# Tokens put in order by the copy out of the attention's banks, and one store per output tile or quarter in place of two

## The chip, the cores and the metric

The kernel runs on one core of a Trainium2 chip. The metric is the device time of one execution in microseconds. Three runs of the kernel before gave 297.45 us as their median (295.93 to 299.62).

## The reference

A retention layer (attention with a decay in place of the softmax) feeds a feed-forward layer with a sine in it. Eight batches of eight heads, 576 tokens each, head width 64; the feed-forward layer has width 512 in and out and 2048 inside.

```
scores = (1/8) * q @ k.T                                  # per batch and head, 576 x 576
gamma[h] = 1 - 2 ** (-5 - h)
ret = scores * where(i >= j, gamma[h] ** (i - j), 0)
attn = ret @ v                                            # 576 x 64 per head
x = attn.transpose(0, 2, 1, 3).reshape(4608, 512)         # heads side by side, one row per token
h = x @ w_in                                              # 4608 x 2048
g = h + sin(alpha * h) ** 2 / (alpha + 1e-9)
out = g @ w_out                                           # 4608 x 512, float32
```

Inputs and output are float32; inside, the matmuls take 16-bit operands and add up in 32 bits.

## The kernel before, in words

The 576 tokens of a batch are two blocks (p = 0, 1) of 256 tokens and an end of 64. The ends of all eight batches are gathered to a ninth block of 512 tokens (class `Ends`), which the feed-forward layer takes as n = 8; n = 0 to 7 are the 512 tokens of batch n's two blocks.

**Token order.** A load of q, k or v of a block (line 158) puts two neighbouring tokens, r = 0 and 1, side by side on one partition, so that the DMA moves longer runs: partition 64 g + i holds the tokens 128 g + 2 i + r. The attention therefore works on tokens in the order (g, r, i): first a half's 64 even tokens, then its 64 odd ones. From batch 4 on (`HALVED`), k and v are loaded in another order (line 153), and half of the masked scores' columns for r = 1 are left out (`i0` = 32 in `scores` and `values`).

**Attention.** `scores` fills a PSUM tile, `masked` multiplies it with the mask into a 16-bit tile, `values` (matmul at line 427) multiplies with v, and `add_states` (line 449) adds what the earlier chunks of 128 tokens contribute through their running state. Both write the tile `o`: two banks (t = 0, 1) of 512 columns, each 2 x 2 x 128 for head pair x, half g and 128 tokens (r, i). They are matmuls of 64 x 64 that use a quarter of the array each. `keep` copies a block's two banks to `xT`, the feed-forward layer's 16-bit input, with ScalarE (line 120) or VectorE (line 122). Columns keep their order on the way.

**Feed-forward layer.** `project` (line 562) makes 16 chunks of 128 hidden features per block, `sine` and `square` (lines 570 and 579 on ScalarE, 581 on the others) and `product` (line 586, VectorE) make `gT`, and the second product follows. For n = 0 to 2 that is `gemm2` (line 605), one tile of 128 tokens by 512 columns at a time, copied out and stored by `finish`. For n = 3 to 8 it is seven products instead of eight in Strassen's manner (`part_product`, line 671; sums at lines 642 and 652), whose results are quarters of 256 tokens by 256 columns, added up on VectorE (line 718) and stored by `store`.

**Stores.** A tile of 128 output rows has the even tokens on its first 64 partitions and the odd ones on the others. So `finish` (line 598) and `store` (line 688) start two transfers each, one for r = 0 and one for r = 1, each to every second row of the output. For n = 8 the two halves belong to different batches (line 684).

**Order of the work.** It is written out by hand, instruction by instruction, for the first three blocks, and as lists of steps per unit for the others. All loads, all transposes by DMA (line 230) and nearly all stores are issued by SP, in program order. Eight completion semaphores are used in turn for these transfers, so that each one waits for the transfer eight places before it. The tile `osb`, from which the stores read, has four buffers.

Of the kernel before, what the change touches and what calls it, by code (L numbers as in the profile page):

```python
# [10 lines left out]
F32 = mybir.dt.float32  # L11
# [25 lines left out]
def kernel(  # L37
# [18 lines left out]
    nc = tc.nc  # L56

    B, H, S, D = q.shape
    DM, FF = moe_w_in.shape
    NT = out.shape[0]  # L60
    P = 128
# [23 lines left out]
    work = ctx.enter_context(tc.tile_pool(name="w", bufs=1))  # L85
# [29 lines left out]
    def halves(n):  # L115
        return slice(64 * n, 64 * n + 64)

    def copy(eng, d_, s_):
        if eng is nc.scalar:
            eng.copy(d_, s_)  # L120
        else:
            eng.tensor_copy(d_, s_)  # L122
# [136 lines left out]
    def change_rows(key):  # L259

        if key in open_turns:
            nc.tensor.drain()
            open_turns.clear()

    def order(later, earlier):
        tc.add_manual_dep(
            later.ins,
            earlier.ins.name,
            mybir.DependencyInfo(mybir.DependencyClass.Sync, mybir.DependencyReason.DATA),
            reason="rows of the two halves take turns at a bank",  # L270
        )

    def told(last, eng):

        mark = eng.nop()
        order(mark, last)
        return mark

    class Attention:
        def __init__(self, b):  # L280
            self.b = b
            self.halved = b >= HALVED
            self.both = {}
            self.o = {}
            self.ret = {}
            self.sc = {}
            self.kv = {}
            self.tiles = {}
            self.mark = {}
# [115 lines left out]
        def values(self, p, same, *tags, relay=None):  # L405

            if same:
                change_rows((self, p))
            else:
                if relay is None:  # L410
                    open_turns.append((self, p))
                if len(tags) == 2:
                    self.o[p] = [psum.tile([P, 512], F32, tag=tag, bufs=1, name="o") for tag in tags]
                else:
                    self.both[p] = psum.tile([P, 2, 512], F32, tag=tags[0], bufs=1, name="o")
                    self.o[p] = [self.both[p][:, t] for t in range(2)]
            o, v16 = self.o[p], half[self.b, "v", p]
            made = []
            for x in range(2):
                for r in range(2):  # L420
                    i0, n = (32, 64) if self.halved and r else (0, 128)
                    for e in range(2):
                        for g in range(2):
                            t = g if same else 1 - g
                            c = 256 * x + 128 * g
                            m = 256 * e + 128 * r
                            made.append(matmul(
                                o[t][halves(e), c : c + 128].rearrange("p (r i) -> p r i", r=2)[:, :, i0:64],
                                v16[halves(g), 4 * t + 2 * x + e, r, :],
                                self.ret[p, x][halves(g), t, m : m + n],  # L430
                                start=(not same and x == 0 and r == 0), stop=False, skip_group_check=True,
                            ))
            if not same and relay is not None:
                self.mark[p] = told(made[-1], relay)
            elif p in self.mark:
                order(made[0], self.mark[p])

        def add_states(self, p, gs=(0, 1)):
            o, qT = self.o[p], T[self.b, "q", p]
            for g in gs:  # L440
                if 2 * p + g == 0:
                    continue
                st = self.state_of(2 * p + g - 1)
                for x in range(2):
                    for e in range(2):
                        for t in range(2):
                            a = 2 * x + e
                            c = 256 * x + 128 * g
                            matmul(
                                o[t][halves(e), c : c + 128],  # L450
                                st[halves(t), a, :],
                                qT[halves(t), 2 * a : 2 * a + 2, halves(g)],
                                start=False, stop=True, skip_group_check=True,
                            )

        def keep(self, p, *engs):

            cols = slice(256 * p, 256 * p + 256)
            if len(engs) == 1:
                copy(  # L460
                    engs[0],
                    self.x[:, :, cols].rearrange("p (t x) n -> p t x n", t=2),
                    self.both[p].rearrange("p t (x n) -> p t x n", x=2),
                )
                return
            for t, eng in enumerate(engs):
                copy(eng, self.x[:, 2 * t : 2 * t + 2, cols], self.o[p][t].rearrange("p (x n) -> p x n", x=2))

    class Ends:

# [75 lines left out]
    ops = {}  # L546
# [38 lines left out]
        hps, ss_t = hps_of.pop((n, fc))  # L585
        nc.vector.scalar_tensor_tensor(gT[n][:, fc, :], ss_t, inva[:, fc : fc + 1], hps, MULT, ADD)  # L586

    def rows_of(n, c):
        if n == 8:
            return out.rearrange("(b s) d -> b s d", s=S)[2 * c : 2 * c + 2, 512:576, :]  # L590
        r0 = 576 * n + 128 * c
        return out[r0 : r0 + 128, :].rearrange("(i r) d -> r i d", r=2)

    def finish(n, c, eng=None, cols=slice(0, 512), issue=(nc.sync, nc.sync)):
        osb = work.tile([P, 512], F32, tag="osb", bufs=4, name="osb")
        copy(eng or nc.scalar, osb[:, cols], ops[n, c, cols.start][:, cols])
        for r in range(2):
            issue[r].dma_start(rows_of(n, c)[r, :, cols], osb[halves(r), cols])

    def gemm2(n, u, tag, cols=slice(0, 512)):  # L600
        c, part = divmod(u, 4)
# [74 lines left out]

    def store(n, t, e, osb, js=(0, 1), issue=(nc.sync, nc.sync)):
        cols = slice(256 * e, 256 * e + 256)
        for r in range(2):
            if n == 8:  # L680
                b0 = 4 * t + 2 * js[0]
                dst = out.rearrange("(b s) d -> b s d", s=S)[b0 : b0 + 2 * len(js), 512:576, cols]
                dst = dst.rearrange("(j r) s d -> r s j d", r=2)
                issue[r].dma_start(dst[r], osb[halves(r), js[0] : js[-1] + 1])
            else:
                r0 = 576 * n + 256 * t + 128 * js[0]
                dst = out[r0 : r0 + 128 * len(js), cols].rearrange("(j i r) d -> r i j d", r=2, i=64)
                issue[r].dma_start(dst[r], osb[halves(r), js[0] : js[-1] + 1])

    kept = {}  # L690

# [8 lines left out]
    def after_product(n, i, js=(0, 1), issue=(nc.sync, nc.sync), apart=False, more=False):  # L700
        acc = parts[n, i]
        if i == 1:
            nc.scalar.copy(kept_tile("low"), acc)
        elif i == 6:
            nc.vector.tensor_tensor(kept_tile("mid"), acc, kept["low"], ADD)
        elif i == 7:
            nc.vector.tensor_tensor(kept["low"], acc, kept["mid" if apart else "low"], ADD)
        else:
            t, e = {2: (0, 0), 3: (0, 1), 4: (1, 0), 5: (1, 1)}[i]
            cols = slice(256 * js[0], 256 * js[-1] + 256)  # L710
            if (n, i) not in kept:
                kept[n, i] = work.tile([P, 2, 256], F32, tag="osb", bufs=4, name="osb")
            osb = kept[n, i].rearrange("p j d -> p (j d)")
            source = kept["mid" if i == 3 else "low"]
            if i == 2 and not apart:
                nc.scalar.copy(osb[:, cols], acc[:, cols])
            else:
                nc.vector.tensor_tensor(osb[:, cols], acc[:, cols], source[:, cols], ADD)  # L718
            store(n, t, e, kept[n, i], js, issue)
            if more:  # L720
                nc.vector.tensor_tensor(kept["mid"], acc, kept["mid"], ADD)
# [60 lines left out]
    with tc.manual_schedule():  # L782
# [222 lines left out]
        load(4, "v", 0)  # L1005
        load(3, "q", 1)
        finish(0, 1)
        at[1].to_state(2, A_)
        finish(0, 3)
        at[1].values(1, True)  # L1010
        at[1].add_states(1)
# [393 lines left out]
        n = NBLK - 1  # L1405
# [50 lines left out]
```

## Time and profile before

| | |
|---|---|
| median of three runs | 297.45 us (295.93 to 299.62) |
| the profiled execution | 296.62 us |
| its span | 294.9 us |
| TensorE (PE), VectorE (DVE), ScalarE (ACT), GpSimd (POOL) busy | 283.0, 225.4, 204.1, 135.8 us |
| granted TensorE clock | 1.0 |
| written to and read from HBM | 9.44 MB, 36.75 MB |
| stores of 128 KB issued by SP | 67 |

PE stands for matmuls, PEld for weight loads beside them. L427 is line 427 of the kernel. SPq is SP's queue of transfers; the time of an issue there is that of the issuing instruction, not of the transfer. In a row of a group, the number behind "x" is the count, then come the busy time of all and the mean of one in ns, and behind the second bar the idle time ahead of them. In a row of waits "A <- B: 1.4, 1, 1.4" A waited for B, 1.4 us in total, once, at most 1.4 us.

### The profile page before, as it was taken

How to read it: one execution, taken by the hardware profiler on the slowest of the kernel's cores; microseconds unless marked ns; L12 is line 12 of the kernel's file. 1: busy time of each engine (PE TensorE's matmuls, PEld its weight loads, DVE VectorE, ACT ScalarE, POOL GpSimd, SP SyncE). 2: the span in 40 equal slices, each digit the busy share in tenths (PEclk: the TensorE clock that was granted, in tenths of full speed). 3: DMA queues.
4: the chain of work that ended last, by engine and by line, in shares of the span. 5: the costliest groups of instructions: out<-in, count | busy, mean ns of one | idle time of the engine just before them, and what ended most of it. 6: DMA issues, size and time to landing. Idle time of an engine off the chain costs nothing. (4 is left out here: it accounts for less than half of the span.)

```text
span 294.9 us, 8502 instructions
## 1 busy us (share of the span) xinstructions
PE 283.0 (96%) x3480; PEld 183.2 (62%) x3480; DVE 225.4 (76%) x336; ACT 204.1 (69%) x341; POOL 135.8 (46%) x151
## 2 busy tenths in 40 slices
PE   6789999999998999999999999999999999999994
PEld 4556545555544554455767766776667776777783
DVE  2586978788347979687987698769877987987884
ACT  2668935998594796787866986688668657765510
POOL 5684678655687684570298129802970000000000
PEclk9999999999999999999999999999999999999999
DMA  7999999998798778997987968798764103110313
GB/s 218 347 234 211 246 291 317 263 261 232 172 204 187 166 165 179 256 174 166 162 192 207 171 148 196 212 147 168 181 151 113 40 10 81 36 38 21 83 39 109
DMA packets 123431, 50.09 MB, mean 170 GB/s; under 512 B 80384, under 2 KB 121344, under 8 KB 123392
## 3 DMA queue, kind: packets, MB, share of 16 engines
q1 hardware_dynamic: 119440, 44.78, 65.5%
q0 software_dynamic: 2688, 4.19, 7.8%
q10 hardware_dynamic: 1264, 0.58, 0.7%
q8 instruction: 27, 0.44, 0.6%
q14 instruction: 12, 0.10, 0.1%
HBM read 36.75 MB, written 9.44 MB: 157 GB/s over the span
## 5 line engine op out<-in xcount | busy, mean ns | idle before, releaser
L586 DVE SCALAR_TENSOR_TENSOR gT<-ss,inva,hps 128x512 f16<-128x512 f16 x144 | 105.6, 744 | 31.5 <-ACT ss L579 27.9
L570 ACT ACTIVATE s<-hps,alpha_t 128x512 f16<-128x512 f32 x144 | 96.8, 680 | 47.1 <-PE hps L562 46.7
L562 PE MATMUL hps<-xT,w_in 128*128 128x512 f16 (+1 forms) x532 | 121.1, 372 | 0.8 <-DMA w_in<-in_moe_w_in_dram 0.8
L562 PEld LDWEIGHTS <-w_in 128*128 128x128 f16 x596 | 66.6, 114 | 50.2 <-DMA w_in<-in_moe_w_in_dram 1.1
L579 ACT ACTIVATE ss<-s 128x512 f16<-128x512 f16 x107 | 67.2, 630 | 2.8
L605 PE MATMUL ops<-w_out,gT 128*128 128x512 f16 x192 | 46.8, 380 | 0.0
L671 PEld LDWEIGHTS <-gT 128*128 128x128 f16 x384 | 37.5, 98 | 8.3
L207 POOL TENSOR_TENSOR k<-raw,cn 128x1024 f16<-128x1024 f32 (+1 forms) x17 | 29.5, 1738 | 9.1 <-DMA raw<-in_k_dram 9.0
L671 PEld LDWEIGHTS <-S 128*128 128x128 f16 x288 | 27.7, 98 | 5.3
L605 PEld LDWEIGHTS <-gT 128*128 128x128 f16 x192 | 17.9, 98 | 20.4
L359 POOL TENSOR_TENSOR s<-kvs,cn 128x256 f16<-128x256 f32 x17 | 10.4, 612 | 40.1 <-DVE S L652 36.6
L207 POOL TENSOR_TENSOR q<-raw,cn 128x1024 f16<-128x1024 f32 x13 | 24.6, 1900 | 7.1 <-DMA raw<-in_q_dram 4.7
L671 PE MATMUL hps<-T,gT 128*128 128x256 f16 x192 | 22.9, 273 | 0.0
L671 PE MATMUL hps<-w_out,gT 128*128 128x256 f16 x192 | 22.9, 273 | 0.0
L671 PE MATMUL hps<-w_out,S 128*128 128x256 f16 x192 | 22.8, 273 | 0.0
L397 DVE TENSOR_TENSOR ret<-sc,mask 128x1024 f16<-128x1024 f32 x16 | 19.1, 1218 | 2.3 <-PE sc L385 2.2
L367 POOL TENSOR_TENSOR kvs<-s,kvs 128x256 f32<-128x256 f32 x21 | 16.7, 797 | 3.6 <-DVE kvs L122 1.1
L718 DVE TENSOR_TENSOR osb<-hps,low 128x512 f32<-128x512 f32 x13 | 9.0, 691 | 9.6 <-PE hps L671 9.6
L581 DVE TENSOR_TENSOR ss<-s 128x512 f16<-128x512 f16 x29 | 13.4, 465 | 3.7 <-ACT s L570 3.7
L366 POOL TENSOR_TENSOR s<-kvs,cn 128x256 f32<-128x256 f32 x21 | 12.9, 612 | 6.8 <-ACT kvs L120 6.6
L652 DVE TENSOR_TENSOR S<-gT,S 128x1024 f16<-128x1024 f16 x24 | 15.5, 684 | 0.0
L397 DVE TENSOR_TENSOR ret<-sc,mask_halved 128x768 f16<-128x768 f32 x16 | 15.2, 950 | 0.0
(83 smaller groups left out, 269.5 us busy)
## 6 DMA issues: line engine op xcount, KB each, us to landing
out_dram<-osb SPq DMA_DIRECT2D x67, 128.0 KB, 2.5
raw<-in_q_dram SPq DMA_DIRECT2D x16, 512.0 KB, 5.1
raw<-in_k_dram SPq DMA_DIRECT2D x8, 512.0 KB, 6.1
raw<-in_v_dram SPq DMA_DIRECT2D x8, 512.0 KB, 6.0
raw<-in_v_dram SPq DMA_DIRECT2D x32, 128.0 KB, 3.3
raw<-in_k_dram SPq DMA_DIRECT2D x32, 128.0 KB, 3.1
w_in<-in_moe_w_in_dram POOLq DMA_DIRECT2D x4, 512.0 KB, 11.9
w_out<-in_moe_w_out_dram POOLq DMA_DIRECT2D x4, 512.0 KB, 13.2
```

The source lines that it names most:

```text
L207: eng.tensor_tensor(dst[:, a0:a1].rearrange("p a r t d -> p t (a r) d"), t_.rearrange("p (t a) x -> p t a x", t=2)[:, :, a0:a1].rearrange( ...
L366: nc.gpsimd.tensor_tensor(s32, self.kvs[:, c - 1], g1.unsqueeze(2).to_broadcast([P, 4, D]), MULT)
L367: nc.gpsimd.tensor_tensor(self.kvs[:, c], s32, self.kvs[:, c], ADD)
L397: nc.vector.tensor_tensor(ret.rearrange("p t (z x) -> p (t z) x", z=2)[:, :, 0:n], sc.rearrange("p t (z x) -> p (t z) x", z=2)[:, :, 0:n], ...
L562: matmul(hps_of[n, fc][0][:, cols], w_in16[fc // 4][:, a, fc % 4 :: 4], xs[n][:, a, cols], start=(a == 0 and part != 1), stop=(a == KT - 1 ...
L570: nc.scalar.activation(s_t, hps, mybir.ActivationFunctionType.Sin, bias=0.0, scale=alpha_t[:, fc : fc + 1],)
L579: nc.scalar.activation(ss_t, s_t, mybir.ActivationFunctionType.Square)
L581: eng.tensor_tensor(ss_t, s_t, s_t, MULT)
L586: nc.vector.scalar_tensor_tensor(gT[n][:, fc, :], ss_t, inva[:, fc : fc + 1], hps, MULT, ADD)
L605: matmul(ops[n, c, cols.start][:, cols], gT[n][:, fk, c * P : (c + 1) * P], w_out16[:, fk, cols], start=(fk == 0), stop=(fk == FC - 1), sk ...
L652: return eng.tensor_tensor(out_, x, y, op)
L671: matmul(acc[:, 256 * j : 256 * j + 256], lhs[:, x, 128 * j : 128 * j + 128], rhs[:, x], start=(tag is not None and j == js[0] and p == 0 ...
```

## The change

A new function `columns` gives the half g and head pair x of a bank a new place: the bank's 256 columns of a head pair are now ordered (r, g, i) instead of (g, r, i). `values` and `add_states` write their 128 columns through it, as two runs of 64 that lie 128 apart. `keep` reads runs of 128 columns (n = 64 g + i) and writes column n of r to place 2 n + r, so that `xT` holds the tokens in their own order. From there on a tile of 128 rows is 128 rows of the output one after the other, and `finish` and `store` start one transfer of 256 KB each. For n = 8 the two transfers stay.

```
+    def columns(bank_, x, g, e):
+        mine = bank_[halves(e), 256 * x : 256 * x + 256]
+        return mine.rearrange("p (r g i) -> p g r i", r=2, g=2)[:, g]
...
                             t = g if same else 1 - g
-                            c = 256 * x + 128 * g
                             m = 256 * e + 128 * r
                             made.append(matmul(
-                                o[t][halves(e), c : c + 128].rearrange("p (r i) -> p r i", r=2)[:, :, i0:64],
+                                columns(o[t], x, g, e)[:, :, i0:64],
...
                             a = 2 * x + e
-                            c = 256 * x + 128 * g
                             matmul(
-                                o[t][halves(e), c : c + 128],
+                                columns(o[t], x, g, e),
...
                 copy(
                     engs[0],
-                    self.x[:, :, cols].rearrange("p (t x) n -> p t x n", t=2),
-                    self.both[p].rearrange("p t (x n) -> p t x n", x=2),
+                    self.x[:, :, cols].rearrange("p k (n r) -> p k r n", r=2),
+                    self.both[p].rearrange("p t (x r n) -> p (t x) r n", x=2, r=2),
                 )
                 return
             for t, eng in enumerate(engs):
-                copy(eng, self.x[:, 2 * t : 2 * t + 2, cols], self.o[p][t].rearrange("p (x n) -> p x n", x=2))
+                copy(
+                    eng,
+                    self.x[:, 2 * t : 2 * t + 2, cols].rearrange("p x (n r) -> p x r n", r=2),
+                    self.o[p][t].rearrange("p (x r n) -> p x r n", x=2, r=2),
+                )
...
-    def finish(n, c, eng=None, cols=slice(0, 512), issue=(nc.sync, nc.sync)):
+    def finish(n, c, eng=None):
         osb = work.tile([P, 512], F32, tag="osb", bufs=4, name="osb")
-        copy(eng or nc.scalar, osb[:, cols], ops[n, c, cols.start][:, cols])
-        for r in range(2):
-            issue[r].dma_start(rows_of(n, c)[r, :, cols], osb[halves(r), cols])
+        copy(eng or nc.scalar, osb, ops[n, c, 0])
+        r0 = 576 * n + 128 * c
+        nc.sync.dma_start(out[r0 : r0 + 128, :], osb)
...
     def store(n, t, e, osb, js=(0, 1), issue=(nc.sync, nc.sync)):
         cols = slice(256 * e, 256 * e + 256)
-        for r in range(2):
-            if n == 8:
...
+        if n == 8:
...
+            for r in range(2):
                 issue[r].dma_start(dst[r], osb[halves(r), js[0] : js[-1] + 1])
-            else:
-                r0 = 576 * n + 256 * t + 128 * js[0]
-                dst = out[r0 : r0 + 128 * len(js), cols].rearrange("(j i r) d -> r i j d", r=2, i=64)
-                issue[r].dma_start(dst[r], osb[halves(r), js[0] : js[-1] + 1])
+        else:
+            r0 = 576 * n + 256 * t
+            nc.sync.dma_start(out[r0 : r0 + 256, cols].rearrange("(j p) d -> p j d", p=P), osb)
```

More of the change, by code (lines that the diff above doesn't have):

```diff
@@ L586, in product @@
         nc.vector.scalar_tensor_tensor(gT[n][:, fc, :], ss_t, inva[:, fc : fc + 1], hps, MULT, ADD)
-    def rows_of(n, c):
-        if n == 8:
-            return out.rearrange("(b s) d -> b s d", s=S)[2 * c : 2 * c + 2, 512:576, :]
+    def finish(n, c, eng=None):
+        osb = work.tile([P, 512], F32, tag="osb", bufs=4, name="osb")
+        copy(eng or nc.scalar, osb, ops[n, c, 0])
         r0 = 576 * n + 128 * c
-        return out[r0 : r0 + 128, :].rearrange("(i r) d -> r i d", r=2)
-    def finish(n, c, eng=None, cols=slice(0, 512), issue=(nc.sync, nc.sync)):
-        osb = work.tile([P, 512], F32, tag="osb", bufs=4, name="osb")
-        copy(eng or nc.scalar, osb[:, cols], ops[n, c, cols.start][:, cols])
-        for r in range(2):
-            issue[r].dma_start(rows_of(n, c)[r, :, cols], osb[halves(r), cols])
+        nc.sync.dma_start(out[r0 : r0 + 128, :], osb)
     def gemm2(n, u, tag, cols=slice(0, 512)):
@@ L678, in store @@
         cols = slice(256 * e, 256 * e + 256)
-        for r in range(2):
[L680 to L683, printed above, removed]
+        if n == 8:
+            b0 = 4 * t + 2 * js[0]
+            dst = out.rearrange("(b s) d -> b s d", s=S)[b0 : b0 + 2 * len(js), 512:576, cols]
+            dst = dst.rearrange("(j r) s d -> r s j d", r=2)
+            for r in range(2):
                 issue[r].dma_start(dst[r], osb[halves(r), js[0] : js[-1] + 1])
-            else:
-                r0 = 576 * n + 256 * t + 128 * js[0]
-                dst = out[r0 : r0 + 128 * len(js), cols].rearrange("(j i r) d -> r i j d", r=2, i=64)
-                issue[r].dma_start(dst[r], osb[halves(r), js[0] : js[-1] + 1])
+        else:
+            r0 = 576 * n + 256 * t
+            nc.sync.dma_start(out[r0 : r0 + 256, cols].rearrange("(j p) d -> p j d", p=P), osb)
     kept = {}
```

## The prediction

> **What bounds the kernel now.** I read the page's span and engine rows first, then the busy time of each engine by stage, then what TensorE waited for, then the timelines of SP, GpSimd and TensorE around the one wait that was found.
>
> ```profile
> span 294.9 us, 8502 instructions
> ...
> PE 283.0 (96%) x3480; PEld 183.2 (62%) x3480; DVE 225.4 (76%) x336; ACT 204.1 (69%) x341; POOL 135.8 (46%) x151
> ...
> 0.00:21.00 21.00, 15.28 (x300) 11.20 (x300) 12.52 (x24) 10.86 (x18) 14.89 (x24) 1.00 1.04 269
> 21.00:75.00 54.00, 53.44 (x733) 30.55 (x734) 42.70 (x63) 40.03 (x66) 33.74 (x35) 1.00 1.05 256
> 75.00:92.00 17.00, 15.62 (x102) 7.62 (x101) 7.54 (x12) 11.88 (x25) 13.07 (x12) 1.00 0.89 196
> 92.00:265.00 173.00, 172.77 (x2144) 113.44 (x2142) 141.51 (x206) 131.63 (x217) 74.06 (x83) 1.00 0.69 147
> 265.00:295.00 30.00, 25.90 (x206) 20.38 (x204) 21.14 (x34) 9.67 (x16) 0.00 (x0) 1.00 0.23 62
> ```
>
> A stage row gives its length, then busy time of PE, PEld, DVE, ACT and POOL, the granted clock (1.00 throughout) and the share of the DMA engines. PE's idle time is the length less the first busy number: 5.72 us in the start, 0.56 until 75 us, 1.38 between 75 and 92 us, 0.23 in the 173 us after that, 4.10 in the end. So TensorE sets the pace from 21 us on, and no edit of transfers or copies gains more than 0.56 + 1.38 + 0.23 = 2.17 us there. The start lies before the first store, and the stores of the last block (n == 8), which end the run, stay as they are: I leave both ends at nothing.
>
> What made PE wait between 21 and 290 us:
>
> ```profile
> PE sc L385 <- DMA qT<-q: 1.4, 1, 1.4
> PE hps L562 <- DMA w_in<-in_moe_w_in_dram: 0.8, 1, 0.8
> ```
>
> The second is a weight load ahead of all stores. The first is the wait of the stage 75 to 92 us. The three engines' timelines there (start, length, instructions):
>
> ```profile
> 68.36 4.25 SPq L598 DMA_DIRECT2D out_dram<-osb  x6
> ...
> 75.54 1.23 SPq L598 DMA_DIRECT2D out_dram<-osb  x2
> 76.87 2.99 SPq L153 DMA_DIRECT2D raw<-in_k_dram  x4
> 80.37 0.40 SPq L158 DMA_DIRECT2D raw<-in_q_dram  x1
> 80.88 2.76 SPq L230 DMA_TRANSPOSE kT<-k  x1
> ...
> 85.02 2.10 SPq L230 DMA_TRANSPOSE qT<-q  x1
> ...
> 76.18 1.06 ACT L120 CAST v<-raw 128x1024 f16<-128x1024 f32 x1
> ...
> 77.75 3.76 POOL L207 TENSOR_TENSOR q<-raw,cn 128x1024 f16<-128x1024 f32 x2
> ...
> 85.20 3.62 PE L605 MATMUL ops<-w_out,gT 128*128 128x512 f16 x16
> 90.19 0.64 PE L385 MATMUL sc<-qT,kT 64*64 64x128 f16 x32 [1.38 <-DMA qT<-q]
> ```
>
> SP issues one transfer behind the other here with hardly a gap. The scores of batch 3 need the transpose that SP issues at 85.02; TensorE is through with its other work at 88.8 us and starts at 90.19.
>
> **The stores.** Twelve tiles (n = 0 to 2, `finish`) and twenty quarters (n = 3 to 7, `store`) lose one of two transfers each: 32 issues on SP's queue. The order of all other instructions on the five engines stays.
>
> ```profile
> L688 SPq DMA_DIRECT2D out_dram<-osb x40: 595/610/1255, 152.2 to 278.3; - x40
> L598 SPq DMA_DIRECT2D out_dram<-osb x24: 517/592/1720, 68.4 to 146.0; - x24
> ...
> DMA to landing us min/median/max: 2.3/2.5/4.9
> ...
> L230 SPq DMA_TRANSPOSE qT<-q x12: 1242/1314/2476, 54.9 to 199.7; - x12
> ```
>
> 12 x 0.592 + 20 x 0.610 = 19.3 us of SP's issue time go, nearly all of it beside TensorE, so they are worth only what PE waited for SP. Of the eight stores ahead of the late transpose four go: three from the first row (3 x 4.25/6 = 2.1 us) and one from the third (0.6 us), together 2.7 us. May SP run that far ahead? The load at 80.37 waits for ScalarE's cast of v, over at 77.24, so it may start at 77.7. The transpose needs GpSimd's second cast of the row at 77.75, over at 81.5, so it may start at 82.3. Both conditions hold, so the transpose can land about 2.7 us earlier, at 87.5, ahead of the 88.8 at which TensorE comes for it. Gain: 1.38 us. The bounds are 0 (what shortens ahead of it is given back, since the issues at 80.88 and 85.02 took 2.76 and 2.10 us where the median transpose of q takes 1.31, so SP was perhaps held by the transfers in flight) and the whole 2.17 us of idle time. What is late next is the transpose of the other half of q of batch 3, which SP issues behind one more store pair; SP is further ahead there than TensorE would be, so I add nothing.
>
> A store of 256 KB instead of 128 KB is one issue with twice the rows. Its issue is bounded by 0.52 us (the shortest store) and by two of the old ones, 1.2 us; I take 0.6, because the issues with 64 and with 128 rows stand at 0.592 and 0.610. Its landing lies between the old store's 2.5 us and a 512 KB load's:
>
> ```profile
> raw<-in_k_dram SPq DMA_DIRECT2D x8, 512.0 KB, 6.1
> ```
>
> Who waits for a landing? The buffer `osb`, one of four, is rewritten a whole block later, and the program uses eight completion semaphores in turn, so each transfer waits for the one eight places before it. Eight issues with their gaps last 8 x 4.25/6 = 5.7 us, and loads of 6.1 us pass through the same ring now. I add nothing; if a store took as long as such a load, SP would stand for 6.1 - 5.7 = 0.4 us behind it, and TensorE not at all.
>
> **The copies.** `keep` now writes its 16-bit result with a step of two elements. The copies, and the nearest others (mean ns of one behind the bar):
>
> ```profile
> L120 ACT CAST xT<-o 128x1024 f16<-128x1024 f32 x10 | 10.1, 1018 | 0.0
> L120 ACT COPY kvs<-kv 128x512 f32<-128x512 f32 x9 | 5.2, 587 | 3.3 <-PE kv L321 2.7 <-PE o L427 0.6
> L120 ACT CAST xT<-o 128x512 f16<-128x512 f32 x5 | 2.8, 593 | 1.2 <-PE o L449 1.2
> L122 DVE CAST xT<-o 128x512 f16<-128x512 f32 x5 | 3.4, 686 | 0.1
> L122 DVE COPY osb<-ops 128x512 f32<-128x512 f32 x2 | 1.4, 686 | 2.3 <-PE ops L605 2.3
> L122 DVE CAST xT<-o 128x1024 f16<-128x1024 f32 x1 | 1.2, 1223 | 1.3 <-PE o L449 1.3
> ```
>
> No row has a step of two 2-byte elements. The nearest ones write 4-byte elements side by side, so 512 elements lie at the same pitch as they will now: 587 against 593 ns on ScalarE, 686 against 686 on VectorE. I take 0. The lower bound is 0 too, since nothing is taken off the copies; the upper one is a doubling, 10.1 + 2.8 + 3.4 + 1.2 = 17.5 us over two engines. On TensorE that would cost only where it comes at once for the copy:
>
> ```profile
> 19.40 1.27 DVE L122 CAST xT<-o 128x512 f16<-128x512 f32 x2
> 21.16 1.06 PE L562 MATMUL hps<-xT,w_in 128*128 128x256 f16 x8 [0.77 <-DMA w_in<-in_moe_w_in_dram]
> ...
> 48.90 1.00 ACT L120 CAST xT<-o 128x1024 f16<-128x1024 f32 x1
> 50.49 1.68 PE L562 MATMUL hps<-xT,w_in 128*128 128x512 f16 x7
> ```
>
> Batch 0: the pair would end about 22.1 instead of 20.67, 0.9 us after 21.16. Batch 1: 50.9 against 50.49, 0.4 us. Behind the later copies TensorE has other work first. Together 1.3 us.
>
> **The matmuls.** `values` and `add_states` now write two runs of 64 columns, 128 apart, instead of 128 in one run. No instruction is added. The rows:
>
> ```profile
> L427 PE MATMUL o<-ret,v 64*64 64x128 f16 x384 | 10.7, 221 | 0.5
> L449 PE MATMUL o<-qT,s 64*64 64x128 f16 x192 | 6.0, 218 | 0.1
> L427 PE MATMUL o<-ret,v 64*64 64x64 f16 x128 | 4.5, 190 | 0.0
> L385 PE MATMUL sc<-qT,kT 64*64 64x64 f16 x128 | 3.7, 189 | 0.0
> ...
> 100.13 1.38 PE L427 MATMUL o<-ret,v 64*64 64x128 f16 x64
> 101.34 0.51 PE L449 MATMUL o<-qT,s 64*64 64x128 f16 x24
> ```
>
> 384 + 192 = 576 matmuls change. The 128 of line 427 with 64 columns already write two runs, of 32 columns 64 apart (the half-masked batches, `i0` = 32), and take 190 ns; the same size of line 385, in one run, takes 189. So I take 0. The Trainium skill says otherwise: its page "PSUM — Partial Sum Buffer", section "Specifications (TRN2)", gives 8-byte cachelines there and has any non-contiguous pattern slow matmuls significantly. By that rule the attention's matmuls would stretch and the sum would be a loss instead of a gain; the rows of lines 427 and 385 speak against it at runs of 32.
>
> **Sum.** The profiled execution took 296.62 us, 1.72 us around its span. 296.62 - 1.38 + 0 + 0 = 295.2. It lies 0.83 us below the median of the runs shown, 297.45 (295.93 to 299.62); carried to a median that is 297.45 - 1.38 = 296.1, which I forecast.
>
> **Rivals.** A: nothing moves. SP gets ahead, but the transpose lands as late as before, because a transfer's landing is bound by the traffic (0.89 of the DMA engines in that stage), or TensorE waits as long at the next transpose. For it: SP's two long transposes. Against it: bytes and packets of the stores are unchanged, and they come earlier. 297.4 us.
>
> B, on the other side: the split output slows the 576 matmuls. 64 of them took 101.34 - 100.13 = 1.21 us, 19 ns each as four tiles of the array work together. If the second run costs as much again, 576 x 19 ns = 10.9 us on the bound engine: 297.4 + 10.9 = 308.3 (307 if the wait goes as well). It passes 2% (5.9 us) from 10 ns per matmul on. Against it stands the pair 190 and 189 ns.
>
> C: strided copies take up to double: +1.3 us, which eats the gain: 297.4 us. Against it: the equal rows at the same pitch.
>
> D: more is gained than TensorE's idle time between 21 and 265 us, over 2%. Nothing in the stage rows leaves room for it; below 291.5 us.
>
> **How the numbers follow.** Forecast (295 to 297) 0.57, A 0.26, C 0.06, B 0.08, D 0.03. All but B and D lie within 2%, about what a measurement of this kernel can tell from no change: same 0.89, slower 0.08, faster 0.03. The range goes from the lowest run shown less the largest gain, 295.93 - 2.17 = 293.8, to the highest run shown with no gain, 299.6; it holds A and C and leaves out B and D.
>
> **What would show it.** Stores: 12 at line 598 and 20 at the line of `store`, about 0.6 us each, 256 KB. The wait of `sc` for `qT` at 88 us gone or under 0.3 us, and 75 to 92 us with PE idle below 0.5 us. Copies to xT at 1.0 and 0.6 us on ScalarE, 0.69 on VectorE. Values and states at 215 to 225 ns, and 64 in a row in about 1.2 us. The prediction is wrong if PE's busy time grows (B), if the copies grow and `project` waits for them (C), or if a transfer waits where none did.

## The result, and the profile after

The changed kernel takes 296.39 us (median of 20 runs, 295.34 to 298.54), the kernel before took 298.55 us beside it (20 runs, 295.71 to 300.0). The ratio is 0.994, with a 95% interval of 0.9917 to 0.9963: a gain of 0.4 to 0.8%, within the 2% that count as no change. A second measurement of the same code gave 296.65 us (12 runs, 295.24 to 297.92) against 297.33, a ratio of 0.9975 (0.9951 to 1.0). The forecast was 296.1 us. The ratios here are worked out from fast runs alone (at most 1.5% above the fastest of the same kernel), so they need not be the quotient of the medians.

The profiled execution of the first measurement happened to be the slowest of its 20 runs, 298.54 us, so a profile of the second one (296.89 us, span 295.2) stands beside it below, as the second profile. First the page of the first profile: the span, the engines' busy time, and the granted clock in 40 slices.

```profile
span 296.8 us, 8464 instructions
PE 284.6 (96%) x3480; PEld 183.6 (62%) x3480; DVE 227.5 (77%) x336; ACT 207.3 (70%) x341; POOL 136.0 (46%) x151
PEclk9999997999999999999999999999999999999999
```

The count of matmuls is that of before, 3480. The seventh slice has a lower clock; before had none. The same run by stage (length, busy time of PE, PEld, DVE, ACT and POOL, granted clock, DMA share, GB/s), and a stretch of 3.4 us within the first of these stages:

```profile
21.00:75.00 54.00, 51.68 (x578) 28.85 (x579) 41.40 (x58) 39.34 (x66) 32.41 (x34) 0.97 1.05 255
75.00:92.00 17.00, 16.91 (x228) 8.82 (x230) 8.30 (x14) 13.08 (x27) 12.47 (x11) 1.00 0.89 202
...
47.60:51.00 3.40, 3.30 (x50) 1.59 (x51) 0.37 (x1) 2.12 (x6) 3.40 (x3) 0.51 1.05 311
```

PE's idle time between 75 and 92 us is 17.00 - 16.91 = 0.09 us where it was 1.38. That looks like the forecast gain and is not. This run lost 54.00 - 51.68 = 2.32 us before 75 us, where it was 0.56, and its clock was halved from 47.6 to 51.0 us, which costs about another 1.7 us (an estimate: half of 3.4). So TensorE comes for the transpose at 91.89, 3.1 us later than the 88.8 of before, while SP issues it only 0.46 us earlier than before (85.02):

```profile
84.56 2.65 SPq L230 DMA_TRANSPOSE qT<-q  x1
...
91.89 0.64 PE L389 MATMUL sc<-qT,kT 64*64 64x128 f16 x32
```

The second profile does show the gain in this place: 0.06 us idle, with 108 matmuls in the stage, about the 102 of before (the first profile has 228).

```profile
75.00:92.00 17.00, 16.94 (x108) 8.13 (x106) 8.37 (x11) 12.73 (x27) 14.50 (x13) 1.00 0.87 201
```

The longest row of what PE waited for between 21 and 292 us in the first profile:

```profile
PE kv L325 <- ACT v L120: 2.0, 1, 2.0
```

The wait of 2.0 us is at 44 us, for a cast of v behind a load. No store has been issued by then (the first is at 69.8 us), and the second profile of the same code has nothing of it. (Three profiles of the experiments below, with the sums moved, the columns' order made by the matmul and the step on the read, have 0.8 to 1.0 us of it; what decides this stays open.) The longest row of the second profile:

```profile
PE hps L568 <- DVE ret L401: 1.1, 1, 1.1
```

In neither profile do the scores wait for `qT`. In the second one there is a new wait of 1.1 us, for `ret` of VectorE, at 92 us; the experiments come back to it. Over the stretch from 21 to 265 us PE is idle for 244.00 - 241.66 = 2.34 us there, against 2.17 before, and the span is 0.3 us longer than that of the profile before (295.2 and 294.9). So these profiles show that a wait went, and not that the kernel became faster: that stands in the times alone.

The stores in the first profile (ns of one issue on SP's queue: shortest, median, longest), and from its page the transfers with KB of each and median us to landing:

```profile
L687 SPq DMA_DIRECT2D out_dram<-osb x20: 372/384/585, 153.2 to 279.5; - x20
...
L598 SPq DMA_DIRECT2D out_dram<-osb x12: 332/530/1450, 69.8 to 147.1; - x12
```

```profile
out_dram<-osb SPq DMA_DIRECT2D x32, 256.0 KB, 2.8
```

And the groups of the copies and of the attention's matmuls (mean ns of one behind the bar), first in the first profile, then in the second, in which no half clock falls on them:

```profile
L120 ACT CAST xT<-o 128x1024 f16<-128x1024 f32 x10 | 13.1, 1322 | 1.8 <-PE o L451 1.8
L120 ACT CAST xT<-o 128x512 f16<-128x512 f32 x5 | 3.6, 743 | 0.9 <-PE o L451 0.9
L122 DVE CAST xT<-o 128x512 f16<-128x512 f32 x5 | 3.6, 733 | 0.6 <-ACT xT L120 0.5
L122 DVE CAST xT<-o 128x1024 f16<-128x1024 f32 x1 | 1.3, 1310 | 3.5 <-PE o L451 3.5
...
L430 PE MATMUL o<-ret,v 64*64 64x64 f16 x128 | 4.3, 190 | 0.0
```

```profile
L430 PE MATMUL o<-ret,v 64*64 64x128 f16 x384 | 10.4, 221 | 0.5
L451 PE MATMUL o<-qT,s 64*64 64x128 f16 x192 | 5.9, 218 | 0.0
```

The matmuls with two runs of 64 columns take what they took with one run of 128, 221 and 218 ns. The copies do not: 1018 became 1322 ns and 593 became 743 on ScalarE (30 and 25% longer), 686 became 733 and 1223 became 1310 on VectorE (7%). That is 10 x 0.304 + 5 x 0.150 + 5 x 0.047 + 0.087 = 4.1 us more of engine time, none of which is seen in PE's waits.

### The profile page after: what moved, and what is told of

It is laid out like the page before. It is cut to its first block, busy times and chain, and to the rows that moved or that the text cites. A ratio compares the mean times of both kernels' runs of the same rounds, so it can differ in the third digit from the quotient of the medians.

```text
span 296.8 us, 8464 instructions
## 1 busy us (share of the span) xinstructions
PE 284.6 (96%) x3480; PEld 183.6 (62%) x3480; DVE 227.5 (77%) x336; ACT 207.3 (70%) x341; POOL 136.0 (46%) x151
## 5 line engine op out<-in xcount | busy, mean ns | idle before, releaser
L605 PE MATMUL ops<-w_out,gT 128*128 128x512 f16 x192 | 47.6, 385 | 0.0
L207 POOL TENSOR_TENSOR k<-raw,cn 128x1024 f16<-128x1024 f32 (+1 forms) x17 | 28.9, 1703 | 7.5 <-DMA raw<-in_k_dram 7.5
L207 POOL TENSOR_TENSOR q<-raw,cn 128x1024 f16<-128x1024 f32 x13 | 24.6, 1903 | 4.5 <-DMA raw<-in_q_dram 4.3
L371 POOL TENSOR_TENSOR kvs<-s,kvs 128x256 f32<-128x256 f32 x21 | 16.0, 762 | 5.5 <-ACT kvs L120 2.8
L120 ACT CAST xT<-o 128x1024 f16<-128x1024 f32 (+1 forms) x15 | 16.5, 1129 | 2.7 <-PE o L451 2.7
L587 DVE TENSOR_TENSOR ss<-s 128x512 f16<-128x512 f16 x29 | 14.3, 495 | 3.0 <-ACT s L576 2.8
```

Of the source, the lines that this page charges most:

```text
L207: eng.tensor_tensor(dst[:, a0:a1].rearrange("p a r t d -> p t (a r) d"), t_.rearrange("p (t a) x -> p t a x", t=2)[:, :, a0:a1].rearrange( ...
L371: nc.gpsimd.tensor_tensor(self.kvs[:, c], s32, self.kvs[:, c], ADD)
L587: eng.tensor_tensor(ss_t, s_t, s_t, MULT)
L605: matmul(ops[n, c, cols.start][:, cols], gT[n][:, fk, c * P : (c + 1) * P], w_out16[:, fk, cols], start=(fk == 0), stop=(fk == FC - 1), sk ...
```

## The experiments

Theory T, the prediction's: what the change is worth is PE's wait for one transpose of q at 88 us, and it goes because SP issues fewer stores ahead of that transpose. Rivals: the stores don't matter (A), the split output costs (B), the copies cost (C).

**Copies and matmuls alone; one store for n = 0 alone; two stores for n = 0 alone.** The token order of the changed kernel stays in all three. What differs is where two stores go out again: for all n from 0 to 7 in the first, for n = 1 to 7 in the second, for n = 0 in the third, which leaves line 687 with one store. The edit of the second:

```
         r0 = 576 * n + 128 * c
-        nc.sync.dma_start(out[r0 : r0 + 128, :], osb)
+        if n > 0:
+            for r in range(2):
+                nc.sync.dma_start(out[r0 + 64 * r : r0 + 64 * r + 64, :], osb[halves(r)])
+        else:
+            nc.sync.dma_start(out[r0 : r0 + 128, :], osb)
...
+            dst = out[r0 : r0 + 256, cols].rearrange("(j p) d -> p j d", p=P)
+            for r in range(2):
+                nc.sync.dma_start(dst[halves(r)], osb[halves(r)])
-            nc.sync.dma_start(out[r0 : r0 + 256, cols].rearrange("(j p) d -> p j d", p=P), osb)
```

> The banks' new order and the copies with a step of two as in the changed kernel, but two stores per tile or quarter again (64 rows each). Theory 1 (the gain is SP's shorter queue ahead of the late transpose of q of batch 3): ratio to the kernel before 1.000, within 0.997 to 1.003, the wait of the scores near 88 us is back at 1 us or more, the copies at 1.3 and 0.74 us on ScalarE cost nothing on TensorE. Theory 2 (the gain comes with the order of the output rows or with the banks' new order): 0.994. Theory 3 (the longer copies cost time that the stores win back): 1.002 to 1.005.

> As the changed kernel, but only the four tiles of n = 0 are stored with one transfer each; the other 28 tiles and quarters keep two. These four are the stores that stand ahead of the late transpose. Theory 1: the whole gain, ratio 0.994 (0.992 to 0.997), no wait of the scores near 88 us. Theory 2 (every store that goes gives a little, through less traffic of issues over the whole run): 4 of 32 parts of the gain, 0.999.

> The counterpart: the four tiles of n = 0 keep two stores, all others have one. Theory 1: no gain, ratio 1.000 (0.997 to 1.003), the wait near 88 us at 1 us or more. Theory 2: 28 of 32 parts of the gain, 0.995.

Measured: the copies and matmuls alone 297.85 us, ratio 0.9986 (0.9953 to 1.002); one store for n = 0 296.69 us, 0.9974 (0.9944 to 1.0004), a little above the 0.997 expected; two stores for n = 0 297.5 us, 1.0014 (0.9974 to 1.0055). The longest row of PE's waits in each, in this order:

```profile
PE sc L389 <- DMA qT<-q: 1.9, 1, 1.9
```

```profile
PE hps L568 <- DVE ret L401: 0.7, 1, 0.7
```

```profile
PE sc L389 <- DVE T L646: 2.4, 1, 2.4
```

The third row names VectorE, but it is the same matmul in the same place, and the transpose that it needs was issued late there. Issue of that transpose in the second and third of them (start, length):

```profile
83.18 1.41 SPq L230 DMA_TRANSPOSE qT<-q  x1
```

```profile
86.03 1.98 SPq L230 DMA_TRANSPOSE qT<-q  x1
```

So the wait at 88 us hangs on four stores of one block, n = 0, whatever the other 28 stores do. With one store each it is shorter, but it does not always go. Leaving out the two kernels below that are much slower, there are seven profiles with one store there. Four show no wait (one of them, the first profile, because TensorE was late) and three show 0.6, 0.9 and 0.9 us: the kernels below with the square moved, with the sums moved and one store for n = 0 only, and with the step on the read. The four profiles with two stores or with padding show 1.4 to 2.4 us. The row of the last two of the three:

```profile
PE sc L389 <- DMA qT<-q: 0.9, 1, 0.9
```

The order of the copies by itself brings nothing that can be measured. The intervals of the times overlap; it is the waits that tell the kernels apart.

The first of these profiles shows a second price of such a wait. Two neighbouring stretches of 3.4 us (columns as above):

```profile
87.50:90.90 3.40, 1.49 (x37) 0.81 (x36) 2.32 (x4) 1.10 (x5) 2.15 (x2) 1.00 1.10 239
91.00:94.40 3.40, 3.40 (x9) 1.21 (x8) 2.16 (x3) 0.16 (x1) 3.24 (x5) 0.50 0.72 175
```

PE was idle for 3.40 - 1.49 = 1.91 us, and then its clock was halved for 3.4 us, which costs about 1.7 us more by the same estimate. The first profile of the changed kernel has the same after its wait of 2.0 us at 44 us. Not every long wait is followed by it: the 2.4 us with two stores for n = 0 and the 2.3 us with padding (below) were not. In every trace the times at which the granted clock changed lie whole multiples of 3.41 us apart. If each run is divided at these times, the two falls came after stretches in which PE was idle for 1.91 and 1.96 us. The wait of 2.37 us is cut in two, 0.95 and 1.42 us, and that of 2.30 us into 0.41 and 1.89. So idle time within one stretch fits better than the length of a wait, with an edge near 1.9 us; it is not settled, since a stretch with 1.95 us idle in the run with all copies twice was not followed by a fall. The Trainium skill, page "TensorE: Matmul & The Clock Gate", section "What's actually happening", describes free-running windows of 3413 ns and has the clock fall after an idle one of them. The length of 3.4 us agrees with these rows, but an idle time of 1.9 us was followed by the fall here, so that a gap well short of a whole window is not safe.

**An earlier transpose in place of fewer stores.** The kernel before, with SP's order changed by hand:

```
         cast(4, "k", 0, G_, (0,))
+        crossed(3, 1, "q")
         wait_for_w_in(3)
         load(4, "q", 0)
-        crossed(3, 1, "q")
```

> The kernel before, with the late transpose of q of batch 3 issued ahead of the wait for the weights and the load of q of batch 4 in SP's queue, which brings it about 1.3 us forward; stores and copies as before. Theory 1: most of the gain without any change of a store, ratio 0.995 (0.993 to 0.998), the wait of the scores near 88 us under 0.5 us. Theory 2: 1.000.

A miss: 297.65 us, ratio 1.0016 (0.9978 to 1.0054). Its waits of PE, and GpSimd's cast that comes after the load which was moved back:

```profile
PE hps L562 <- DVE gT L586: 1.7, 2, 0.9
PE sc L385 <- DMA qT<-q: 1.0, 1, 1.0
```

```profile
91.42 1.91 POOL L207 TENSOR_TENSOR q<-raw,cn 128x1024 f16<-128x1024 f32 x1 [1.88 <-DMA raw<-in_q_dram]
```

The wait at 88 us went, but the load behind which the transpose used to stand now lands late, GpSimd waits 1.88 us for it, the other half of q is late (the 1.0 us, at 97 us), and two waits for `gT`, 0.9 us at 94 us and 0.8 us at 116 us, are not in the profile before (the second stands in several profiles below too). Turning the order round moved the wait in this one try; other orders weren't tried.

**The changed kernel again, and the same with something put back in the queue.** The second adds, behind each store of n = 0, a small transfer that nothing waits for:

```
         nc.sync.dma_start(out[r0 : r0 + 128, :], osb)
+        if n == 0:
+            pad = work.tile([P, 64], F16, tag=f"pad{c}", bufs=1, name="pad")
+            nc.sync.dma_start(pad, zero[:, 0:64])
```

> The changed kernel once more, as the measure for the three others and as a second profile. Theory 1: ratio to the kernel before 0.994 (0.991 to 0.998), no wait of the scores for a transpose near 88 us, PE idle under 0.5 us from 75 to 100 us.

> The changed kernel with one more small transfer (128 x 64 in SBUF, which nothing waits for) issued by SP behind each of the four stores of n = 0. Theory 1 (SP's issues and semaphore turns ahead of the late transpose count, not what they move): the wait near 88 us is back at about 1 us or more, ratio 1.000 (0.996 to 1.003). Rival (the gain lies in the stores themselves, their 128 partitions, their rows one after the other or their landing): 0.994, no wait.

With the padding 297.01 us, 1.0013 (0.998 to 1.0046), and the wait is back:

```profile
PE sc L389 <- DMA qT<-q: 2.3, 1, 2.3
```

So it is the issues in SP's queue that make the transpose late, not the stores' rows or bytes. Whether it is the time of the issues or the turns of the eight semaphores that they take, this run does not separate. The changed kernel again gave 0.9975 and the second profile above. PE was idle there for 1.10 us from 75 to 100 us, where under 0.5 was expected. SP's queue in it, ahead of the transpose of q:

```profile
68.00 2.55 SPq L598 DMA_DIRECT2D out_dram<-osb  x3
...
74.08 0.57 SPq L598 DMA_DIRECT2D out_dram<-osb  x1
...
78.33 0.54 SPq L158 DMA_DIRECT2D raw<-in_q_dram  x1
78.97 2.64 SPq L230 DMA_TRANSPOSE kT<-k  x1
...
83.30 2.19 SPq L230 DMA_TRANSPOSE qT<-q  x1
```

The load goes out 2.0 us ahead of before (80.37), the transpose 1.7 us (85.02). What PE, VectorE and GpSimd did then, and the same cast and square in the kernel before:

```profile
88.62 0.64 PE L389 MATMUL sc<-qT,kT 64*64 64x128 f16 x32
...
93.01 1.02 PE L568 MATMUL hps<-xT,w_in 128*128 128x512 f16 x4 [1.05 <-DVE ret L401]
...
88.65 2.16 DVE L587 TENSOR_TENSOR ss<-s 128x512 f16<-128x512 f16 x1
90.73 1.10 DVE L642 TENSOR_TENSOR T<-w_out 128x1024 f16<-128x1024 f16 x1
91.75 1.21 DVE L401 TENSOR_TENSOR ret<-sc,mask 128x1024 f16<-128x1024 f32 x1
...
88.62 1.90 POOL L207 TENSOR_TENSOR q<-raw,cn 128x1024 f16<-128x1024 f32 x1 [1.31 <-DMA qT<-q]
```

```profile
88.86 0.42 DVE L581 TENSOR_TENSOR ss<-s 128x512 f16<-128x512 f16 x1
...
90.13 1.90 POOL L207 TENSOR_TENSOR q<-raw,cn 128x1024 f16<-128x1024 f32 x1 [2.40 <-DMA qT<-q]
```

GpSimd's next cast of q starts as soon as the transpose has read the buffer, so its start marks the landing: 88.62 instead of 90.13 us, 1.5 us earlier and just in time for PE. But there the cast meets a square of VectorE, which ends with it and takes 2.16 us instead of 0.42. The sum and the mask behind it are late, and PE waits 1.05 us for the mask's product. Most of the 1.38 us that were gained at 88 us is given back at 92 us in this profile. The square is held up in the same way wherever it runs beside a cast of q: in eight profiles it took 0.83 to 2.16 us and ended 0.27 to 0.30 us behind the cast, and in three where no cast ran beside it (the kernel before, padding, the step on the read) it took 0.42 us.

**Taking that square off VectorE.** The changed kernel, with the square on ScalarE; then the same with two sums of VectorE moved earlier too, from behind products of n = 2; then that with one store for n = 0 only. The first has only the two lines with the square, the others all:

```
         gemm2(1, 7, "h0")
+        weight_sum("T3", 0, V)
+        weight_sum("T3", 1, V)
         finish(1, 1, V)
...
         at[3].to_state(0, A_)
+        square(2, 3, A_)
         sine(2, 4)
...
         product(2, 0)
-        square(2, 3, V)
-        weight_sum("T3", 0, V)
         at[3].masked(1, 1)
         product(2, 3)
-        weight_sum("T3", 1, V)
```

> The changed kernel with one square of block 2 (chunk 3) done by ScalarE, which is idle then, instead of VectorE. Theory 1b: with the wait for the transpose gone, this square starts together with GpSimd's cast of q and takes 2.16 us instead of 0.42, VectorE comes late to the bank that project waits for, and 1.1 us of the gain is given back at 91 us. Then here: no 16-bit VectorE operation over 1.5 us between 88 and 93 us, the wait of project at 91 us under 0.6 us, PE idle from 75 to 100 us about 0.6 us instead of 1.1, ratio 0.992 to 0.996. Rival (VectorE's work there is too much by itself): the wait stays at 1 us, ratio as the changed kernel's.

> As square_moved, and the two sums of weights T3 move from 90 to 94 us to VectorE's idle time at 75 us. Theory 1b: PE idle from 75 to 100 us under 0.4 us, 0.7 us or more less than the changed kernel, ratio to the kernel before 0.990 to 0.995. Rival: no gain over the changed kernel, since VectorE then delays the copies of batch 2 at 78 us.

> As sums_early, but only the four tiles of n = 0 are stored with one transfer, the others with two as before. In the profiles so far the kernels with one store for n = 1 to 7 had PE idle for 0.5 to 1.1 us from 100 to 265 us, those with two 0.1 us, because SP further ahead lets a cast on GpSimd meet VectorE's sums of weights at 112 us. If that holds: PE idle from 100 to 265 us 0.2 us or less, about 0.5 us less than sums_early, ratio 0.989 to 0.994. If the later stores do not matter: as sums_early within the noise, and 0.5 us or more idle from 100 to 265 us in either.

Measured: 296.14 us, 0.9949 (0.9918 to 0.9981); 295.94 us, 0.9955 (0.9925 to 0.9984); 296.45 us, 0.9977 (0.9946 to 1.0009). In the first, PE's longest wait and VectorE's sum that was 1.10 us long:

```profile
PE sc L389 <- DMA qT<-q: 0.6, 1, 0.6
```

```profile
88.90 0.69 DVE L642 TENSOR_TENSOR T<-w_out 128x1024 f16<-128x1024 f16 x1
```

The wait for `ret` is gone, which fits the collision: without the square VectorE is not held up. It is no clean test by itself, since the transpose landed later in this run, at 89.43 by the cast's start, so that 0.6 us of the old wait is there. The span is 294.1 us, the shortest of all profiles here, but 0.9949 cannot be told from the changed kernel's 0.994 and 0.9975. Moving the sums has no effect that can be told from that either. With the sums moved, another wait stays, for `gT` at 114 us:

```profile
PE hps L568 <- DVE gT L592: 0.8, 1, 0.8
```

It was expected to hang on the single stores of n = 1 to 7. It stands in the third kernel too, which has two stores there (0.8 us), and in those with padding and with the turned order (0.8 us each, at 116 us), and not in the one with one store for n = 0 above. The third kernel was expected to have PE idle for 0.2 us or less from 100 to 265 us and a ratio of 0.989 to 0.994; it had 1.48 us and 0.9977. That expectation fell, and what decides which runs have this wait stays open.

**The columns' order made by the matmul instead of the copy.** The output's step is now one element (8 bytes from column to column) instead of runs of 64, and the copies are those of before:

```
-        mine = bank_[halves(e), 256 * x : 256 * x + 256]
-        return mine.rearrange("p (r g i) -> p g r i", r=2, g=2)[:, g]
+        mine = bank_[halves(e), 256 * x + 128 * g : 256 * x + 128 * g + 128]
+        return mine.rearrange("p (i r) -> p r i", r=2)
```

> The tokens are put in order by the matmuls instead of the copies: values and add_states write every second column of a bank (runs of one element, 8 bytes apart), and the copies read and write side by side as in the kernel before. One store each, as changed. Theory 1 (a split output costs a matmul nothing): lines of values and add_states at 220 ns, 64 of them in 1.2 us, copies back at 1.02 and 0.59 us on ScalarE, ratio 0.994. Rival B of the prediction (output that is not side by side slows the matmuls): 576 x 19 ns = 10.9 us more, ratio 1.03.

304.26 us, ratio 1.0209 (1.0159 to 1.026): slower, though the interval leaves open whether by 2%. PE's busy time and the three groups of matmuls:

```profile
PE 291.7 (97%) x3480; PEld 190.4 (63%) x3480; DVE 226.8 (75%) x336; ACT 204.9 (68%) x341; POOL 137.0 (45%) x151
...
L430 PE MATMUL o<-ret,v 64*64 64x128 f16 x384 | 16.4, 305 | 0.5
L451 PE MATMUL o<-qT,s 64*64 64x128 f16 x192 | 8.4, 309 | 0.0
L430 PE MATMUL o<-ret,v 64*64 64x64 f16 x128 | 6.5, 258 | 0.0
```

A matmul takes 305 ns instead of 221, 309 instead of 218, 258 instead of 190, and PE is busy 291.7 us instead of the 283.0 of before. The rule of the Trainium skill's page "PSUM — Partial Sum Buffer", section "Specifications (TRN2)", that a non-contiguous pattern slows matmuls, holds for single elements. It does not hold for runs of 64 or 32 elements of 4 bytes, which cost nothing (221 and 190 ns).

**Copies with the step on the read.** The copy reads PSUM with the step and writes side by side; nothing else differs:

```
-                    self.x[:, :, cols].rearrange("p k (n r) -> p k r n", r=2),
-                    self.both[p].rearrange("p t (x r n) -> p (t x) r n", x=2, r=2),
+                    self.x[:, :, cols].rearrange("p k (n r) -> p k n r", r=2),
+                    self.both[p].rearrange("p t (x r n) -> p (t x) n r", x=2, r=2),
```

> The changed kernel with the order of the copies' loops turned round: they write their 16-bit results side by side and read the banks with a step instead (alternating between two places 128 columns apart). If the step of the write is what made the copies 30% longer (1.32 against 1.02 us), they are back at 1.02 to 1.05 us and 0.59 us on ScalarE; if any step of one element on either side costs, they stay at 1.3 us or more. On the time of the kernel within 1 us of the changed kernel either way, ratio 0.993 to 1.000.

296.76 us, 0.9979 (0.9947 to 1.0011): no difference from the changed kernel that can be told. But the copies are back at the durations of before:

```profile
L120 ACT CAST xT<-o 128x1024 f16<-128x1024 f32 x10 | 10.1, 1019 | 0.0
...
L120 ACT CAST xT<-o 128x512 f16<-128x512 f32 x5 | 2.8, 593 | 1.3 <-PE o L451 1.3
```

VectorE's are back too (683 and 1225 ns). So it is the written step of two 2-byte elements that costs the 30%; reading PSUM from two places 128 columns apart in turn costs nothing.

**All copies twice.** Every copy of `keep` is made two times. That is more than rival C's doubling: two of the longer copies take 2.6 us where one took 1.02 before.

```
+                for _ in range(2):
                     copy(eng, ...)
```

> The changed kernel with each copy of the attention's result done twice in a row (the same data to the same place). It prices the copies: about 17 us more on ScalarE and 5 us more on VectorE. Theory 1 (the copies lie beside TensorE except in batches 0 and 1): 1 to 2.5 us more than the changed kernel, ratio to the kernel before 0.997 to 1.003. Rival C (the copies are on the path): 16 copies of about 1.3 us, 20 us, ratio 1.06.

312.96 us (308.48 to 313.97), ratio 1.0449 (1.0384 to 1.0515), where at most 1.003 was expected. PE's longest waits, and one of them with the copies ahead of it, in the profiled run (308.48 us):

```profile
PE hps L570 <- ACT xT L120: 7.7, 4, 2.4
PE hps L570 <- DVE xT L122: 3.8, 3, 2.3
```

```profile
167.33 2.67 ACT L120 CAST xT<-o 128x1024 f16<-128x1024 f32 x2
170.33 2.64 ACT L120 CAST xT<-o 128x1024 f16<-128x1024 f32 x2
173.02 1.24 PE L570 MATMUL hps<-xT,w_in 128*128 128x512 f16 x5 [2.43 <-ACT xT L120]
```

The copies end up to 2.4 us after PE is ready for them, in seven places. The 4.1 us of the real change are hidden, but copies of 2.6 times the old length cost ten times the price that was put on a doubling. A doubling itself wasn't run. Here each pair would have taken 2.04 us instead of 2.65, which leaves about 1.2 of the 2.43 us of wait (an estimate).

One store per tile with the old token order wasn't tried, so what the single stores bring without the change of the copies stands open.

## Why the prediction was right

**The bound.** TensorE sets the pace in all profiles, and idle time is what changed hands. This held.

**The stores.** Right in mechanism. The wait at 88 us went or became shorter when SP had fewer issues ahead of the transpose, and came back with two stores or with padding for n = 0 alone. "Together 2.7 us" was too much: the load came 2.0 us and the transpose 1.7 us earlier, and it landed at 88.62 instead of the 87.5 forecast. The gain of 1.38 us in this place is therefore right with almost no margin, not with 1.3 us of it, and three of seven profiles kept 0.6 to 0.9 us of the wait. One term was mis-sized: of "I take 0.6", 256 KB a store, the quarters measured 0.384 us and the tiles 0.53, and so 12 x 0.53 + 20 x 0.384 = 14.0 us of SP's time stand in place of 24 x 0.592 + 40 x 0.61 = 38.6. That is 24.6 us less, not 19.3, and the quarters lie below the bound of 0.52 us that was given. But the issues that count here did not shorten as forecast: the three stores at 68.00 took 2.55 us, 0.85 each, and the transposes at 78.97 and 83.30 are as long as before (2.64 and 2.19 against 2.76 and 2.10 us). A landing of 2.8 us lay in the range given, and no engine waited for one.

**"What is late next ... I add nothing."** This step failed in part. The transpose of the other half of q was not late, as argued. What was late was VectorE, because the cast that the transpose releases on GpSimd now came beside a square. This was not looked for: the prediction followed SP and PE past the moved transfer, but not GpSimd. It costs 1.05 us in one profile, 0.7 in that with one store for n = 0, and nothing that shows in the first profile.

**The copies.** "I take 0" failed: 4.1 us of engine time, since the pitch of 4-byte elements says nothing on a step of 2-byte ones. On the time this had no effect (0.9986 with the copies alone). The price of rival C failed by far: "Behind the later copies TensorE has other work first" is true of copies 30% longer and untrue of copies 2.6 times as long, which cost 13 us of the whole (1.0449 x 297.33 - 297.33) where 1.3 was said for a doubling.

**The matmuls.** Right: 221, 218 and 190 ns, and rival B is out for runs of 64. The pair of rows at runs of 32 was a good guide.

**The median.** 296.39 and 296.65 us against the 296.1 forecast, and a ratio of 0.994 or 0.9975 against 296.1 / 297.45 = 0.9955. Leaving out the kernels with the stepped matmuls and the doubled copies, there are 90 runs of kernels with one store for n = 0, and 161 of the kernel before and of those with two stores, padding or the turned order. Their medians are 296.36 and 297.44 us, 1.1 us apart where 1.38 was forecast.

That the number came so close is in part luck. The sum left out two things of opposite sign. One is the wait at 92 us, which gave back most of the gain in the second profile. The other is the spread: of the 90 runs 1 is above 298.5 us (that of the first profile, with its half clock after the wait at 44 us), of the 161 there are 50. The prediction's upper bound of 2.17 us comes from one profile at full clock and does not hold for runs that lost some of it.

That the long runs have a half clock after the wait at 88 us fits what the first experiment showed, but no profile of theirs shows it. The mean granted clock of a whole run, on record for 141 of the 161 and for all 90, bears it out in part. One stretch of 3.4 us at half clock lowers that mean by 0.006: to 0.993 in the profile of the copies alone, to 0.994 in the first profile. Two stretches at the start of the run make it 0.988, as in the second profile, which was not long for it. Of the 38 runs above 298.5 us among the 141, 31 have a mean of 0.989 to 0.994 or under 0.984, and 4 of the other 103. Of the 90, 5 have. But one stretch at the start gives 0.994 as well (the profile with the step on the read). So the long runs very likely lost their clock in the middle; that the wait at 88 us was the cause in them is argued, not shown.

## What to carry to other kernels

Where one queue issues loads, transposes and stores in program order, look for the one transfer that an engine comes for too early, and count the issues ahead of it: by the waits, four stores decided here, and 28 did not. Then follow what the earlier transfer lets go on every engine, since the work released may meet other work in a new place. Changing the order of columns cost nothing here in runs of 32 or 64 elements of the matmul's output or on the copy's read side, and did cost in its 16-bit write.

## What the runs showed of the hardware

- After an idle time of PE of 1.9 to 2.0 us the granted clock was 0.50 and 0.51 for 3.4 us, in two profiles. After waits of 1.4, 2.3 and 2.4 us in three others it was not. The clock changed only at multiples of 3.41 us from one another in each trace; within one such stretch the idle time was 1.91 and 1.96 us where the fall followed, and 1.38, 1.89 and 1.42 us in those three. One stretch with 1.95 us, in the run with all copies twice, had no fall behind it, so the edge stays open.
- A copy from PSUM whose 16-bit result is written with a step of two elements takes 1322 ns instead of 1018 on ScalarE (128x1024) and 733 instead of 686 on VectorE (128x512). Written side by side, and read in turn from two places 128 columns apart, it takes 1019 and 683 ns.
- A matmul of 64 x 64 with 128 columns takes 221 ns into one run, 221 ns into two runs of 64 columns and 305 ns into single columns 8 bytes apart.
- A 16-bit square of VectorE that takes 0.42 us alone took 0.83 to 2.16 us beside GpSimd's cast of 1.90 us, in eight profiles, and ended 0.27 to 0.30 us behind the cast in each.
- One transfer of 256 KB was issued in 0.384 us (128 partitions, two runs of 256 columns) where each of two transfers of 128 KB took 0.61 (medians).
